# Down projection of the first three row tiles in three accumulation steps each, placed between the products of the inverse transform

## Chip, cores, metric

The kernel runs on one core of one Trainium2 chip. The metric is the device time of one execution in microseconds (us). A profile of one execution per kernel is read beside it; its span is some 2 us shorter than the device time. Within a group of runs the kernels share one chip and the runs of the kernel before.

## The reference

```
xn  = layernorm(x)                            # x: 2048 rows x 640, bf16
A   = irfft2(rfft2(xn) * (w_r + i w_i))       # over rows and columns
B   = ((xn @ w_gate) * (xn @ w_up)) @ w_down  # 640 -> 1536 -> 640
out = x + A + B
```

## The kernel before

The program is a list of tasks with priorities and dependences. A planner in the kernel's own code orders them on each engine at build time and hands out the eight PSUM banks (the buffers into which TensorE writes its sums; a bank is held until ScalarE or VectorE has read it, which is called an eviction where it is a copy); the chip then runs a fixed instruction stream per engine with semaphore waits. A lower priority number goes first; a task of lower priority may go ahead where the other can't start yet. Caps limit how many tasks of a class hold a bank at once.

The stages: layernorm and transposes (to some 20 us); the gate and up products, interleaved with the forward transform and then with the inverse transform along the rows (to some 140 us); the down projection, interleaved with the inverse transform along the columns (to the end). The tasks that the argument touches, cut:

```python
sch.caps = {"glu": 3, "acc": 3, ...}        # gate/up, down projection sums
...
ia = T("IA_%d" % q, "pe", ...)              # L1129, L1130: inverse row transform, 10 matmuls
ti = T("I_%d" % a, "pe", ...)               # L1158: inverse column transform, 5 matmuls, needs all of IA
# L1182 ... L1215: thirteen VectorE instructions per pair of row tiles (tasks V1 to V5)
...
def em_ag2(c, ...):                         # L1241: one sum of the down projection
    for ft in _FT_ORDER:                    # (7, 8, 9, 10, 11, 0, 1, 2, 3, 4, 5, 6)
        ins = c.e.matmul(ps[:, bk, ...], v_ht[:, ft, ...], v_wd[:, ft, sl3], start=(ft == 7 ...), stop=False)
ag2 = T("ACC_%d_%d" % (a, hf), "pe", 12 * ..., em_ag2,
        reads=[(b_ht, ...), (b_wd, None)],  # None: all of w_down
        prio=41 + ..., bank="single", cls="acc")
iv = T("IV_%d_%d", "pe", ..., after=[ag2])  # L1251: last product of a sum, needs V5
f1 = T("FIN_%d_%d", "dve", ..., frees=own, after=[iv])   # L1261: adds x, frees the bank
```

There are 16 row tiles of two halves (the last tile has three pieces), so 33 sums. w_down shares its memory with the table of the inverse row transform, apart from slices 7 to 11.

## Time and profile before

| | before |
|---|---|
| device time, median of the first runs | 207.04 us (206.98 to 207.76) |
| span of the profiled run | 205.3 us (this execution took 207.48) |
| TensorE, share busy | 97% |
| VectorE, share busy | 88% |
| TensorE time with nothing streaming, after the first transpose | 5.5 us: 4.9 in the pieces that the prediction lists, 0.6 in crumbs |

The distance between the starts of two matmuls, less what a fed stream takes (136 ns after one of 320 columns, 216 after 512): such gaps are called holes below. The wait that a profile line shows in brackets is smaller, since a matmul's record includes its pipeline.

### The profile page before, as it was taken

To read this page: it belongs to the slowest core of one execution; us is meant where nothing else is said; L and a number is where in the kernel's file an instruction comes from. 1 tells how busy PE (TensorE), PEld (TensorE's weight loads), DVE (VectorE), ACT (ScalarE), POOL (GpSimd) and SP (SyncE) were. 2 spreads that over 40 slices of the span, in tenths; PEclk is the share of its full clock that TensorE was granted. 3 is DMA by queue.
4 is the path that set the end of the run, shared out by engine and by line. 5 is a ranking of instruction groups with operands and counts; after the bars stand their busy time and mean duration, and the time that the engine had idled before them with its cause. 6 is when DMAs were issued, how large, how long until landed. Compare 5 with 4: busy or idle time off the path is not lost.

```text
span 205.3 us, 5062 instructions
## 1 busy us (share of the span) xinstructions
PE 198.4 (97%) x1925; PEld 134.9 (66%) x1925; DVE 179.7 (88%) x513; ACT 129.5 (63%) x287; POOL 32.2 (16%) x108
## 2 busy tenths in 40 slices
PE   7997999999999999899999999997999999999995
PEld 7897899545454555456666666656777777777774
DVE  3598999999999997697988889865999999999972
ACT  3687999999977676869999999987411220200000
POOL 0000000000000000075754575452000000000000
PEclk9999999999999999999999999999999999999999
DMA  6999963030351897405354534015122422243212
GB/s 182 299 337 382 361 80 64 3 64 0 64 69 36 247 201 203 128 0 133 74 149 104 130 81 118 0 16 159 55 60 84 117 80 67 80 112 111 82 50 64
DMA packets 31543, 23.83 MB, mean 116 GB/s; under 512 B 10528, under 2 KB 29472, under 8 KB 31392
## 3 DMA queue, kind: packets, MB, share of 16 engines
q1 hardware_dynamic: 30720, 23.16, 42.5%
q10 hardware_dynamic: 800, 0.36, 0.6%
q8 instruction: 15, 0.25, 0.5%
q14 instruction: 8, 0.07, 0.1%
HBM read 18.92 MB, written 2.62 MB: 105 GB/s over the span
## 4 chain that ended last, share of the span: by engine, by line
PE 89%; DVE 6%; DMA 1%; issue 1%; POOL 1%; ACT 0%; POOLq 0%
PE ps L977 37%; PE ps L1241 23%; PE ps L997 13%; PE ps L1129 3%; PE ps L1130 2%; PE ps L938 2%; PE ps L1251 2%; PE ps L1078 2%; PE ps L1055 2%; DVE arena L719 2%; PE ps L1158 2%; DMA arena<-in_A_x_dram 1%; PE ps L849 1%; PE ps L738 1%; DVE arena L785 0%
## 5 line engine op out<-in xcount | busy, mean ns | idle before, releaser
L718 ACT ACTIVATE arena<-ps 128x512 bf16<-128x512 f32 (+6 forms) x214 | 105.9, 534 | 40.5 <-PE ps L1158 25.3
L977 PE MATMUL ps<-arena 128*128 128x512 bf16 x360 | 84.1, 379 | 0.1
L977 PEld LDWEIGHTS ps<-arena 128*128 128x128 bf16 x360 | 33.2, 98 | 35.6 <-ACT arena L718 2.1
L1241 PE MATMUL ps<-arena 128*128 128x320 bf16 (+2 forms) x396 | 55.8, 295 | 0.0
L1241 PEld LDWEIGHTS ps<-arena 128*128 128x128 bf16 x396 | 37.9, 98 | 13.8
L997 PE MATMUL ps<-arena 128*128 128x128 bf16 (+1 forms) x360 | 28.0, 237 | 1.2 <-issue 1.1
L997 PEld LDWEIGHTS ps<-arena 128*128 128x128 bf16 x360 | 25.1, 98 | 3.2 <-issue 1.5
L1093 DVE TENSOR_TENSOR arena<-ps,arena 128x256 bf16<-128x256 f32 x64 | 24.0, 416 | 0.1
L1106 POOL TENSOR_SCALAR arena<-arena 128x256 bf16<-128x256 bf16 x8 | 6.8, 856 | 90.4 <-DVE arena L1096 90.4
L1013 DVE TENSOR_TENSOR arena<-arena 128x512 bf16<-128x512 bf16 x36 | 15.2, 422 | 5.0 <-ACT arena L718 4.9
L1261 DVE TENSOR_TENSOR arena<-ps,arena 128x320 bf16<-128x320 f32 (+2 forms) x33 | 15.5, 472 | 3.2 <-PE ps L1251 3.2
L719 DVE CAST arena<-ps 64x321 bf16<-64x321 f32 (+1 forms) x25 | 12.2, 490 | 6.3 <-PE ps L1130 5.9
L1129 PEld LDWEIGHTS ps<-arena 128*128 128x128 bf16 x160 | 12.4, 114 | 3.1 <-ACT arena L718 0.4
L1129 PE MATMUL ps<-arena 128*128 128x64 bf16 x160 | 13.3, 196 | 0.3 <-POOL arena L1115 0.3
L1130 PE MATMUL ps<-arena 128*128 128x64 bf16 x160 | 13.3, 197 | 0.0
L1130 PEld LDWEIGHTS ps<-arena 128*128 128x128 bf16 x160 | 11.2, 114 | 2.0
L1115 POOL TENSOR_SCALAR arena<-arena 128x65 bf16<-128x65 bf16 x32 | 12.0, 376 | 0.0
L1113 POOL COPY arena<-arena 128x63 bf16<-128x63 bf16 x32 | 8.7, 271 | 17.0 <-DVE arena L1096 16.8
L1096 DVE TENSOR_TENSOR arena<-ps,arena 128x130 bf16<-128x130 f32 x32 | 9.3, 291 | 0.0
L776 ACT ACTIVATE arena<-arena 128x640 bf16<-128x640 bf16 x11 | 9.1, 826 | 0.0
L1114 POOL COPY arena<-arena 128x63 bf16<-128x63 bf16 x32 | 8.9, 279 | 0.0
L891 DVE TENSOR_TENSOR arena<-arena 128x384 f32<-128x384 bf16 x16 | 8.8, 552 | 0.0
(63 smaller groups left out, 222.3 us busy)
## 6 DMA issues: line engine op xcount, KB each, us to landing
arena<-in_A_x_dram SPq DMA_DIRECT2D x20, 160.0 KB, 2.5
out_dram<-arena SPq DMA_DIRECT2D x31, 80.0 KB, 1.6
arena<-in_A_w_r_dram SPq DMA_DIRECT2D x8, 160.5 KB, 3.0
arena<-in_A_w_i_dram SPq DMA_DIRECT2D x8, 160.5 KB, 3.1
arena<-in_B_w_gate_dram SPq DMA_DIRECT2D x4, 320.0 KB, 5.6
arena<-in_A_x_dram SPq DMA_DIRECT2D x1, 1280.0 KB, 11.1
arena<-in_A_w_r_dram SPq DMA_DIRECT2D x14, 80.2 KB, 2.8
arena<-in_A_w_i_dram SPq DMA_DIRECT2D x14, 80.2 KB, 2.9
```

Source lines behind the costliest of these rows:

```text
L718: return c.e.activation(dst, src, _ACTF.Copy)
L719: return c.e.tensor_copy(dst, src)
L977: ins = c.e.matmul(ps[:, bk, :], v_gw[:, w, j, ft, :], v_xt[:, j, rows], start=(j == 0), stop=(j == 4))
L997: ins = c.e.matmul(ps[:, bk, w * n:(w + 1) * n], v_gw[:, w, j, ft, :], v_xt[:, j, rows], start=(j == 0), stop=(j == 4))
L1013: return c.e.tensor_tensor(v_ht[:, ft0, rows], v_gbf[:, rr, 0, :], v_gbf[:, rr, 1, :], _OP.mult)
L1093: c.e.tensor_tensor(dst, xh.unsqueeze(1).to_broadcast([128, 2, 32, 4]), wv, _OP.mult)
L1096: return c.e.tensor_tensor(d5, x5, wg[:, :, 0:321:5], _OP.mult)
L1115: return c.e.tensor_scalar(yg[:, 128:193], yg[:, 256:321], -1.0, None, _OP.mult)
L1129: c.e.matmul(dst, l1, v_ti[:, q, 0, :], start=True, stop=False)
L1130: ins = c.e.matmul(dst, l2, v_ti[:, q, 1, :], start=False, stop=True)
L1241: ins = c.e.matmul(ps[:, bk, 0:sl3.stop - sl3.start], v_ht[:, ft, a * 128:(a + 1) * 128], v_wd[:, ft, sl3], start=(ft == 7 and px is None) ...
L1261: return c.e.tensor_tensor(v_out[:, a % 2, sl3], ps[:, bk, 0:sl3.stop - sl3.start], v_xr[:, xs, sl3], _OP.add)
```

## The change

The intent: let the down projection of rows 0 to 2 fill TensorE's holes where the gate and up products have run out and the inverse transform waits for evictions. The diff, cut, without the removed branch for a preloaded x, which was never taken, and without the list of weight steps, which gives the same numbers as the old formula:

```diff
-        sch.caps = {"glu": opts.get("cap_glu", 3), "acc": opts.get("cap_acc", 3), "fill": 1}
+        sch.caps = {"glu": opts.get("cap_glu", 4), "acc": opts.get("cap_acc", 5), "fill": 1}
-            pf = opts.get("f_prio", 6.05) + 0.05 * g
+            pf = opts.get("f_prio", 5.8) + 0.05 * g
 ...
-                ag2 = T("ACC_%d_%d" % (a, hf), "pe", 12 * _d_mm(c1 - c0), em_ag2,
-                        reads=[(b_ht, ("col", a, a + 1)), (b_wd, None)], ...
+                cuts = (0, 5, 9, 12) if a < opts.get("acc_split", 3) else (0, 12)
+                own = ag2 = None
+                for k0, k1 in zip(cuts[:-1], cuts[1:]):
+                    def em_ag2(c, a=a, sl3=sl3, k0=k0, k1=k1, own=own):
+                        bk = bank_of(c.t) if own is None else bank_of(own)
+                        for ft in _FT_ORDER[k0:k1]:
+                            ins = c.e.matmul(..., start=(ft == _FT_ORDER[0]), stop=False)
+                    rd = [(b_wd, ("e", 640 * min(fts), 640 * (max(fts) + 1)))] if k1 - k0 < 12 else [(b_wd, None)]
+                    ag2 = T("ACC_%d_%d_%d" % (a, hf, k0), "pe", (k1 - k0) * _d_mm(c1 - c0), em_ag2, reads=[...] + rd, ...)
 ...
-                       prio=opts.get("iv_prio", 19.0) + ...
+                       prio=opts.get("iv_prio", 5.0) + ...
-        sch.urgent = ('T0_0', 'T0_1', 'T0_2', 'T0_3')
+        sch.urgent = ('T0_0', 'T0_1', 'T0_2', 'T0_3', 'sd_1', 'sd_2', 'sd_3')
```

More of the change, by code (lines that the diff above doesn't have):

```diff
@@ L958, in _build @@
                     q="act" if w_ and i < 1 else "sp")
-        w_at = [6.0 + opts.get("w_rate", 2.2) * min(ft // 2, 4) for ft in range(12)]
+        w_at = [6.0 + opts.get("w_rate", 2.2) * opts.get("w_step", (0, 1, 2, 3, 4, 4))[ft // 2] for ft in range(12)]
         c_at = [6.3 + opts.get("c_rate", 2.6) * (b0 + nb - 1) for b0, nb in _CHUNKS]
@@ L1228, in _build @@
                 sl3 = slice(c0, c1)
-                pre = a >= opts.get("x_pre", 16)
-                px = None
-                if pre:
-                    def em_px(c, xs=xs, sl3=sl3):
-                        return c.e.activation(ps[:, bank_of(c.t), 0:sl3.stop - sl3.start], v_xr[:, xs, sl3], _ACTF.Copy)
-                    px = T("PX_%d_%d" % (a, hf), "act", _d_act(c1 - c0), em_px, reads=[(b_xr, ("r", xs, xs + 1))],
-                           prio=pc + 0.001 * hf, bank="single", cls="acc")
@@ L1237, in em_ag2 @@
-                def em_ag2(c, a=a, sl3=sl3, px=px):
-                    bk = bank_of(c.t) if px is None else bank_of(px)
-                    ins = None
-                    for ft in _FT_ORDER:
-                        ins = c.e.matmul(ps[:, bk, 0:sl3.stop - sl3.start], v_ht[:, ft, a * 128:(a + 1) * 128],
-                                         v_wd[:, ft, sl3], start=(ft == 7 and px is None), stop=False)
-                    return ins
-                kw = dict(bank="single", cls="acc") if px is None else dict(after=[px])
@@ L1245, in _build @@
-                ag2 = T("ACC_%d_%d" % (a, hf), "pe", 12 * _d_mm(c1 - c0), em_ag2,
-                        reads=[(b_ht, ("col", a, a + 1)), (b_wd, None)],
-                        prio=pc + 0.01 + 0.001 * hf, **kw)
-                own = ag2 if px is None else px
+                cuts = (0, 5, 9, 12) if a < opts.get("acc_split", 3) else (0, 12)
[3 more added lines that the diff above has]
+                        bk = bank_of(c.t) if own is None else bank_of(own)
+                        ins = None
+                        for ft in _FT_ORDER[k0:k1]:
+                            ins = c.e.matmul(ps[:, bk, 0:sl3.stop - sl3.start], v_ht[:, ft, a * 128:(a + 1) * 128],
+                                             v_wd[:, ft, sl3], start=(ft == _FT_ORDER[0]), stop=False)
+                        return ins
+                    kw = dict(bank="single", cls="acc") if own is None else dict(after=[ag2])
+                    fts = _FT_ORDER[k0:k1]
+                    rd = [(b_wd, ("e", 640 * min(fts), 640 * (max(fts) + 1)))] if k1 - k0 < 12 else [(b_wd, None)]
+                    ag2 = T("ACC_%d_%d_%d" % (a, hf, k0), "pe", (k1 - k0) * _d_mm(c1 - c0), em_ag2,
+                            reads=[(b_ht, ("col", a, a + 1))] + rd,
+                            prio=pc + 0.01 + 0.001 * hf + opts.get("acc0_prio", 0.0) * (a < opts.get("acc_split", 3)), **kw)
+                    own = own or ag2
@@ L1254, in _build, with em_f1 @@
                        reads=[(b_v, ("a", a, a + 1)), (b_sm, ("t", 1, 3))],
-                       prio=opts.get("iv_prio", 19.0) + 0.05 * a + 0.01 + 0.001 * hf, after=[ag2])
-                def em_f1(c, own=own, a=a, xs=xs, sl3=sl3, pre=pre):
+                       prio=opts.get("iv_prio", 5.0) + 0.05 * a + 0.01 + 0.001 * hf, after=[ag2])
+                def em_f1(c, own=own, a=a, xs=xs, sl3=sl3):
                     bk = bank_of(own)
-                    if pre:
-                        return copy_on(c, v_out[:, a % 2, sl3], ps[:, bk, 0:sl3.stop - sl3.start])
                     return c.e.tensor_tensor(v_out[:, a % 2, sl3], ps[:, bk, 0:sl3.stop - sl3.start], v_xr[:, xs, sl3],
                                              _OP.add)
-                f1 = T("FIN_%d_%d" % (a, hf), ("act", "dve") if pre else "dve",
-                       {"dve": _d_dve_psum(c1 - c0), "act": _d_act(c1 - c0)}, em_f1,
-                       reads=[] if pre else [(b_xr, ("r", xs, xs + 1))], writes=[(b_out, rb[0])],
+                f1 = T("FIN_%d_%d" % (a, hf), "dve", _d_dve_psum(c1 - c0), em_f1,
+                       reads=[(b_xr, ("r", xs, xs + 1))], writes=[(b_out, rb[0])],
                        prio=opts.get("fin_prio", 41.0) + 0.05 * a - 0.001, frees=own, after=[iv])
@@ L1270, in _build @@
         sch.window = 100.0
-        sch.urgent = opts.get("urgent", ('T0_0', 'T0_1', 'T0_2', 'T0_3'))
+        sch.urgent = opts.get("urgent", ('T0_0', 'T0_1', 'T0_2', 'T0_3', 'sd_1', 'sd_2', 'sd_3'))
         sch.slack["act"] = opts.get("slack_act", 700.0)
```

## The prediction

> **What bounds the kernel now.** I read the busy shares of the page first, then the chain that ended last, then the table by stretches of 10 us, then the order of time around each hole in TensorE's row, and last VectorE's row from 140 us to the end. By source line: L997 and L977 are the gate and up products, L1129 and L1130 the inverse row transform, L1158 the inverse column transform, L1182 to L1215 its VectorE part, L1241 the down projection, L1251 the last product added to it, L1261 the addition of x.
>
> Page, parts 1 and 4:
>
> ```profile
> PE 198.4 (97%) x1925; PEld 134.9 (66%) x1925; DVE 179.7 (88%) x513; ACT 129.5 (63%) x287; POOL 32.2 (16%) x108
> ...
> PE 89%; DVE 6%; DMA 1%; issue 1%; POOL 1%; ACT 0%; POOLq 0%
> ```
>
> TensorE is 97% busy and is 89% of the chain. But a matmul's record here includes its pipeline: a 320-column one is recorded as 299 ns while the next starts 136 ns after it. So I took the distances between starts, and subtracted the record less 163 ns, which is what a fed stream shows (216 ns for 512 columns, 136 for 320, 56 for 128, about 30 for 64). What remains is TensorE time with no work streaming. After the first transpose at 5.55 us it is 4.9 us in all: 0.7 in pieces of 0.08 to 0.23 before 15 us; 1.29 at 16.43; 0.71 at 86.32; 0.31 at 94.74; 0.43, 0.78, 0.12 and 0.30 between 139.9 and 142.9; 0.27 at 148.94; the rest in crumbs. From 149 us to 203.0 there is none. Everything else is products that the change keeps.
>
> TensorE in order of time:
>
> ```profile
> 139.96 0.19 PE L1129 MATMUL ps<-arena 128*128 128x64 bf16 x1 [0.27 <-POOL arena L1115]
> ...
> 141.06 2.28 PE L1158 MATMUL ps<-arena 128*128 128x128 bf16 x30 [0.62 <-ACT arena L718]
> 143.22 3.42 PE L1241 MATMUL ps<-arena 128*128 128x320 bf16 x24
> ```
>
> This is the seam between two stages. The gate and up products, which filled the holes of the inverse transform, run out at 139.2 us (the group of ten at 137.04). What is left waits for GpSimd, then for ScalarE's eviction, then for two evictions more inside the 30. The down projection could fill it, but its first matmul stands at 143.22, because each of its tasks asks for all of w_down. That weight shares its memory with the inverse transform's table, so its last slice (160 KB) is issued at 140.48, after the last L1130, and lands at 142.69. The first 800 KB (slices 7 to 11, which share nothing) landed at 82.01; slices 0 to 3 by 127.43; 4 and 5 at 139.96.
>
> The stretches, and VectorE in order of time; columns of the first are busy us of PE, PEld, DVE, ACT, POOL, then clock and DMA:
>
> ```profile
> 130.00:140.00 10.00, 9.73 (x113) 5.91 (x110) 7.39 (x24) 8.87 (x22) 5.57 (x19) 1.00 0.13 34
> 140.00:150.00 10.00, 9.13 (x94) 6.82 (x95) 8.19 (x19) 5.15 (x9) 0.00 (x0) 1.00 0.29 84
> 150.00:160.00 10.00, 10.00 (x88) 7.50 (x87) 10.00 (x26) 2.07 (x4) 0.00 (x0) 1.00 0.30 83
> 160.00:170.00 10.00, 10.00 (x82) 7.38 (x80) 9.97 (x24) 1.83 (x3) 0.00 (x0) 1.00 0.32 91
> ```
>
> ```profile
> 142.10 0.82 DVE L719 COPY arena<-ps 128x640 f32<-128x640 f32 x1 [1.65 <-PE ps L1158]
> ...
> 199.43 0.89 DVE L1261 TENSOR_TENSOR arena<-ps,arena 128x320 bf16<-128x320 f32 x2 [1.29 <-PE ps L1251]
> 201.34 0.49 DVE L1261 TENSOR_TENSOR arena<-ps,arena 128x320 bf16<-128x320 f32 x1 [1.01 <-PE ps L1251]
> 202.38 0.36 DVE L1261 TENSOR_TENSOR arena<-ps,arena 128x192 bf16<-128x192 f32 x1 [0.55 <-PE ps L1251]
> 203.03 0.29 DVE L1261 TENSOR_TENSOR arena<-ps,arena 128x128 bf16<-128x128 f32 x1 [0.30 <-PE ps L1251]
> ```
>
> From 142.10 to 198.14 VectorE has no hole over 0.06 us; only the last four waits, 1.29 + 1.01 + 0.55 + 0.30 = 3.15 us, are slack. So the last stage is nearly two-bound. VectorE finishes a pair of rows every 7.0 us (its last step, L1215, starts at 148.47, 155.49, 162.51, ...), and TensorE's work for a pair is 4 x 13 x 0.136 = 7.07 us.
>
> **What the Trainium skill says.** "Perfetto Trace Analysis", Identifying the Most-Contended Engine: matmul busy share is no good measure of headroom on the tensor engine. The trace agrees (299 ns recorded against 136 ns of spacing), hence the count by starts. The same page, Optimization Strategy: where the most-contended engine changes over time, interleaving the stages may help, and the gaps on that engine are the place to look. That is what this change tries. "TensorE: Matmul & The Clock Gate", Step-by-step: a warm stream spaces matmuls by N/2.4 + 2.5 ns, 135.8 for 320 columns; the trace has 136. "PSUM — Partial Sum Buffer", The four PSUM rules: a sum may be continued later, since only a first matmul clears marks in its own bank. So cutting a group of twelve in three, with each sum in a bank of its own, adds no matmul; the bank is only held longer. No run has shown that yet.
>
> **The change part by part.**
> - *Down projection of rows 0, 1, 2 (six sums) in steps of 5, 4 and 3 matmuls, each asking only for its own slices.* Work added: none; 6 x 12 = 72 matmuls x 0.136 = 9.8 us stay. A step of 5 (0.68 us) can run any time after 82 us, one of 4 (0.54 us) after 127.4, one of 3 (0.41 us) only after 142.7.
> - *Sums in flight 3 to 5.* Before 142.7 us up to 5 x 9 x 0.136 = 6.1 us of filler is thus allowed, against holes of 0.43 + 0.78 + 0.12 + 0.30 = 1.63 us. The fillers come last in priority, so they go where nothing else can start. The later hole of 0.27 is a wait for the first VectorE pair (148.9) with all three banks filled: two more banks close it too. Sum: 1.63 + 0.27 = 1.9 us off TensorE's path.
> - *Gate/up cap 3 to 4.* One more bank for the filler of the middle stage. At most the holes at 86.32 and 94.74, 1.0 us; these follow waits for VectorE's evictions and are where the planner may not have foreseen them. ScalarE is 9.6 of 10 us busy there, so more gate/up products in flight mostly queue for it. I count 0.2.
> - *Priority of the forward transform 6.05 to 5.8.* In the old numbering it already stands just ahead of the layernorm group that it doesn't depend on, and VectorE is 9.7 to 10.0 of 10 us busy from 20 to 80 us either way. I count 0.
> - *Three square roots made urgent.* ScalarE starts them 0.02 to 0.2 us after their input already (7.14, 10.89, 13.36). I count 0. The hole of 1.29 us at 16.43 has no releaser in the profile and the change does not aim at it.
> - *Last product's priority 19 to 5.* It runs as soon as its data are there; this frees a bank sooner. 0 by itself.
> - *The list of weight steps* gives the same numbers as the old formula, and the removed branch for a preloaded x was never taken (its threshold is 16, rows go to 15). 0.
>
> Subtract: up to 0.5 us because an inverse transform's product that becomes ready while a step of 0.41 to 0.68 us runs must wait for it, half of one on average, and because five held banks of eight leave fewer pairs of banks for L1158. That delays VectorE's start at 142.9, not TensorE. VectorE's own floor is 203.0 - 3.15 = 199.9 us for the start of the last addition, plus 0.5 for this delay = 200.4; TensorE's is 203.0 - 1.9 - 0.2 = 200.9. TensorE still decides, narrowly; I take 0.2 off for the friction. Net gain 1.9 + 0.2 - 0.2 = 1.9 us: 207.04 - 1.9 = 205.1.
>
> **Rivals.**
> 1. VectorE becomes the bound. For it: rates of 7.0 and 7.07 us per pair, 10.00 busy. If the new order starts the first pair a microsecond later, the end is 199.9 + 1.0 + friction and the gain shrinks to about 1: 206.0. Against: 3.15 us of slack.
> 2. Five held sums starve the middle stage. If fillers slip in from 86 us on, each keeps its bank until 149 us; 5 of 8 gone leaves 3 for gate/up and transform, and TensorE waits for evictions. That could cost 1 to 3 us: 206 to 208. Against: fillers stand behind the gate/up products, and TensorE is full in 97 to 137 us, so few holes call them.
> 3. The middle stage gains as well. All of the 1.0 us at 86 and 95, and an inverse chain that ends earlier since fillers need no eviction: gain about 3 us, 204.0. Beyond that VectorE's 3.15 us stop it.
> 4. The order of the first 17 us changes by luck of the re-planning: plus or minus 1 us.
>
> **Range and chances.** Best guess 205.1. Rivals 1 and 2 make the upper side, 206.5; rival 3 with luck at the start the lower, 203.8. Faster by over 2% needs under 202.9, 4.1 us, which is nearly all idle time that I can find and more than VectorE's slack, so it takes an earlier VectorE start as well: 4%. Slower by over 2% needs over 211.2: 2%.
>
> **What would show it.** Right: down-projection steps of 5 and 4 between the transform products before 142 us, no hole over 0.2 us in TensorE's starts from 137 to 150 us, the same 1925 matmuls, the last additions waiting for TensorE by under 3.15 us in all. Wrong: the first L1182 of the new kernel over a microsecond later with VectorE full to the end (rival 1); new waits of L977 for evictions between 90 and 137 us (rival 2); or a changed start of the forward transform, which I count as nothing.

## The result, and the profile after

The changed kernel took 205.01 us in the median (204.64 to 205.58, four runs) against 207.09. The ratio was 0.9895, with a 95% interval of 0.9864 to 0.9927. A ratio is the mean time of one kernel's runs over that of the other's of the same rounds, so it is not quite the ratio of the medians quoted. In a later group of five rounds the same two kernels stood at 205.05 and 206.41 us, ratio 0.993 (0.9913 to 0.9946). By the medians the gain is 2.1 us in the first group and 1.4 us in the second; the intervals of both allow 1.5 to 1.8 us. The forecast was 1.9 us and 205.1.

The line numbers of the changed kernel differ from the kernel before past L1226: L1236 is the down projection (was L1241), L1248 the last product (was L1251), L1256 the addition of x (was L1261).

Page, parts 1 and 4, after:

```profile
PE 197.5 (97%) x1908; PEld 134.8 (66%) x1925; DVE 179.5 (88%) x513; ACT 129.5 (64%) x287; POOL 31.9 (16%) x108
...
PE 67%; DVE 20%; DMA 4%; SPq 4%; issue 2%; ACT 2%
```

The shares don't tell the two kernels apart. The number of weight loads is the same, 1925; that only 1908 matmuls are shown is 17 records of L977 missing from this trace, each of which looks like a false gap of 0.215 us and is left out of all sums. The chain now runs through VectorE for 20% instead of 6%. That does not make VectorE the bound: the run with less VectorE work, below, is not faster beyond the noise. The shares also vary for one stream (TensorE 89% in the profile of the kernel before, 82% in the control's).

TensorE in order of time after the change, at the seam between the stages (the start of a piece, its length, engine, line, what it does, how many):

```profile
138.48 0.84 PE L1236 MATMUL ps<-arena 128*128 128x320 bf16 x5
...
139.49 0.71 PE L1236 MATMUL ps<-arena 128*128 128x320 bf16 x4
140.27 1.00 PE L1158 MATMUL ps<-arena 128*128 128x128 bf16 x15
141.10 0.84 PE L1236 MATMUL ps<-arena 128*128 128x320 bf16 x5
141.78 0.44 PE L1158 MATMUL ps<-arena 128*128 128x128 bf16 x5
142.06 0.71 PE L1236 MATMUL ps<-arena 128*128 128x320 bf16 x4
```

The three lines of before have become six. The steps of 5 and 4 of the two halves of row 0 stand in front of and between the products, and no wait is bracketed any more. Of the four holes, 1.63 us in all, 0.24 us is left, before the 15 at 140.27: the filler was finished and the last eviction was not. The hole of 0.27 us before the first last product is gone too. Before, and after:

```profile
148.94 0.58 PE L1251 MATMUL ps<-arena 128*128 128x320 bf16 x3
```

```profile
148.47 0.71 PE L1248 MATMUL ps<-arena 128*128 128x320 bf16 x4
```

But 20 us later there is a new one. ScalarE, TensorE and VectorE, after:

```profile
159.70 1.30 ACT L718 ACTIVATE arena<-ps 128x640 f32<-128x640 f32 x2 [6.73 <-PE ps L1158]
...
163.04 0.71 PE L1248 MATMUL ps<-arena 128*128 128x320 bf16 x4
...
163.47 0.49 DVE L1256 TENSOR_TENSOR arena<-ps,arena 128x320 bf16<-128x320 f32 x1
...
164.03 1.80 PE L1236 MATMUL ps<-arena 128*128 128x320 bf16 x12 [0.28 <-DVE arena L1256]
```

Four last products run at 163.04, VectorE's first addition ends and frees a bank at 163.96, and only then does the next sum start: a hole of 0.44 us. The cap of five is not what stops it. By then 12 sums are complete and eight additions are done, so four sums hold banks; the other four banks were emptied by ScalarE's evictions of L1158, which ended at 161.0. The planner did not use them. For a single bank its code prefers one whose neighbour is held (`pen = 0.0 if partner[0] is None else 1.0`) over one that comes free earlier. Its plan, rebuilt from the kernel's code and not visible in a trace, puts the next sum in the bank that this addition frees.

So the seam and what follows it gained 1.63 - 0.24 + 0.27 - 0.44 = 1.22 us. The two profiles differ by 205.3 - 203.1 = 2.2 us. The remaining 1.0 us lies before 24 us, where the two streams are nearly the same: the first group of ten L938 starts at 23.36 us before and at 22.33 after. Before:

```profile
14.80 0.50 PE L997 MATMUL ps<-arena 128*128 128x128 bf16 x6
16.43 2.74 PE L997 MATMUL ps<-arena 128*128 128x128 bf16 x45 [1.13 <-issue]
```

In the changed kernel's profile this hole isn't there. Comparing the two built programs shows what can differ at all. On every engine the streams are the same up to the last ten L1130, but for one place: near 13 us the urgent square root sd_3 stands before one eviction on ScalarE, and two VectorE instructions change places. Raising the gate/up cap, the forward transform's priority and the last product's priority changed no instruction: with any one of them set back, the changed kernel's program is the same.

The VectorE end of the last stage, after:

```profile
198.73 1.67 DVE L1256 TENSOR_TENSOR arena<-ps,arena 128x320 bf16<-128x320 f32 x4 [1.30 <-PE ps L1248]
200.70 0.29 DVE L1256 TENSOR_TENSOR arena<-ps,arena 128x128 bf16<-128x128 f32 x1 [0.30 <-PE ps L1248]
```

Its slack at the end shrank from 3.15 to 1.60 us.

### The profile page after: what moved, and what is told of

It is laid out like the page before. It is cut to its first block, busy times and chain, and to the rows that moved or that the text cites. A ratio compares the mean times of both kernels' runs of the same rounds, so it can differ in the third digit from the quotient of the medians.

```text
span 203.1 us, 5045 instructions
## 1 busy us (share of the span) xinstructions
PE 197.5 (97%) x1908; PEld 134.8 (66%) x1925; DVE 179.5 (88%) x513; ACT 129.5 (64%) x287; POOL 31.9 (16%) x108
## 4 chain that ended last, share of the span: by engine, by line
PE 67%; DVE 20%; DMA 4%; SPq 4%; issue 2%; ACT 2%
PE ps L1236 26%; PE ps L977 24%; DMA arena<-in_A_x_dram 4%; SPq L712 4%; PE ps L997 3%; PE ps L1130 2%; PE ps L1078 2%; PE ps L1129 2%; PE ps L1158 2%; PE ps L1248 2%; DVE arena L1013 2%; PE ps L1055 2%; DVE arena L902 2%; DVE arena L891 2%; DVE arena L892 1%
## 5 line engine op out<-in xcount | busy, mean ns | idle before, releaser
L977 PE MATMUL ps<-arena 128*128 128x512 bf16 x343 | 81.0, 379 | 1.0
L977 PEld LDWEIGHTS ps<-arena 128*128 128x128 bf16 x360 | 33.1, 98 | 35.6 <-ACT arena L718 2.1
L1236 PE MATMUL ps<-arena 128*128 128x320 bf16 (+2 forms) x396 | 55.8, 295 | 0.3 <-DVE arena L1256 0.3
L1236 PEld LDWEIGHTS ps<-arena 128*128 128x128 bf16 x396 | 37.6, 98 | 14.0 <-DVE arena L1256 0.6
L997 PE MATMUL ps<-arena 128*128 128x128 bf16 (+1 forms) x360 | 28.1, 237 | 0.0
L997 PEld LDWEIGHTS ps<-arena 128*128 128x128 bf16 x360 | 24.9, 98 | 2.2 <-ACT arena L718 0.5
L1256 DVE TENSOR_TENSOR arena<-ps,arena 128x320 bf16<-128x320 f32 (+2 forms) x33 | 15.4, 472 | 1.6 <-PE ps L1248 1.6
L1130 PE MATMUL ps<-arena 128*128 128x64 bf16 x160 | 13.3, 197 | 0.0
L1130 PEld LDWEIGHTS ps<-arena 128*128 128x128 bf16 x160 | 11.2, 113 | 2.1
```

What stands on the lines that cost most here:

```text
L977: ins = c.e.matmul(ps[:, bk, :], v_gw[:, w, j, ft, :], v_xt[:, j, rows], start=(j == 0), stop=(j == 4))
L997: ins = c.e.matmul(ps[:, bk, w * n:(w + 1) * n], v_gw[:, w, j, ft, :], v_xt[:, j, rows], start=(j == 0), stop=(j == 4))
L1130: ins = c.e.matmul(dst, l2, v_ti[:, q, 1, :], start=False, stop=True)
L1236: ins = c.e.matmul(ps[:, bk, 0:sl3.stop - sl3.start], v_ht[:, ft, a * 128:(a + 1) * 128], v_wd[:, ft, sl3], start=(ft == _FT_ORDER[0]), st ...
L1256: return c.e.tensor_tensor(v_out[:, a % 2, sl3], ps[:, bk, 0:sl3.stop - sl3.start], v_xr[:, xs, sl3], _OP.add)
```

## The experiments

Two theories for the 2.2 us between the profiles. Theory A: the seam gives about 1.2 us, and the altered start removes a hole that belongs to the old order. Theory B: the hole at 16.43 us is chance, and the rest of the change must account for everything. Twelve kernels ran, in three groups of four, five rounds each.

### The control: two parts that change no instruction

```diff
 kernel before
-"cap_glu", 3   "f_prio", 6.05
+"cap_glu", 4   "f_prio", 5.8
```

> The kernel before with two parts of the change put in, the gate/up cap at 4 and the forward transform's priority at 5.8. The planner gives the same instruction stream on every engine, so all theories expect a ratio of 1.000 within 0.003. It is the control, and a second look at the hole of 1.29 us at 16.43 us: if the hole belongs to the stream (theory A) it is there again, at 1.1 to 1.4 us in TensorE's starts near 16.4 us; if it is chance of one execution (theory B) it is gone or lies elsewhere.

206.63 us against 206.52, ratio 1.0001 (0.9986 to 1.0016). TensorE in order of time in this run, where the kernel before had the hole:

```profile
14.83 3.39 PE L997 MATMUL ps<-arena 128*128 128x128 bf16 x54
```

The same stream ran on without the stop; its first L938 stands at 22.37 us, as in the changed kernel. So the hole of 1.29 us does not belong to the stream but to one execution (or to its chip, since the two profiles are of different groups), and the profile pair exaggerates the change by about 1 us. On one chip, too, the start varies: this run and the run without the new start, below, have the same stream up to 138 us, and their first L938 stands at 22.37 and 22.92 us. Theory A falls in that point.

The DMA records of the traces hold a candidate that the waits don't show. The first packet of the kind "instruction" on queue 8 (16 KB) after the start stands at 14.07 us in the profile of the kernel before and at 11.34 us in this one. Of the other twelve profiles, five have it at 12.8 to 13.1 us, and four of these have a hole of 0.35 to 0.62 us between two L997 from 15.3 to 15.7 us; seven have it before 12 us, and none of these has such a hole over 0.10 us from 15 to 17 us. No run tests it, so it is not shown as the cause.

### The start alone

```diff
 kernel before
-sch.urgent = (..., 'T0_3')
+sch.urgent = (..., 'T0_3', 'sd_1', 'sd_2', 'sd_3')
```

> The kernel before with only the three urgent square roots. The streams differ in one place: sd_3 on ScalarE comes before one gate/up eviction, and VectorE's two products of that time come after the scaling. Theory A (the old order is what makes the hole at 16.43 us): no hole there, 1.0 us faster, ratio 0.995. Theory B (chance): the same as the control, ratio 1.000. My prediction counted this part as 0, as theory B does.

206.31 us, ratio 0.9986 (0.997 to 1.0002). Its profile had two large holes near the start, 0.41 at 14.22 and 0.79 us at 15.58. The measured effect is 0.3 us; the interval reaches from none to 0.6 us, so it is not separated from zero.

### Everything but the start

```diff
 changed kernel
-sch.urgent = (..., 'T0_3', 'sd_1', 'sd_2', 'sd_3')
+sch.urgent = (..., 'T0_3')      # and cap_glu 3, f_prio 6.05
```

> The changed kernel with the old start (and with the old gate/up cap and forward priority, which change no instruction). What stays is the cut sums, their own slices, and five sums in flight. Theory A: 1.1 to 1.2 us faster than the kernel before, ratio 0.9943, and 1.0 us slower than the changed kernel. Theory B: all of the change's 2.1 us, ratio 0.990. The seam from 137 to 143 us reads as in the changed kernel, with TensorE holes of about 0.25 us instead of 1.63.

205.26 us, ratio 0.9938 (0.9922 to 0.9955): 1.3 us. The holes are 0.24 at 140.85 and 0.44 us at 164.6. The seam's account of 1.22 us from the profile and the measured 1.3 us agree. Theory B's ratio of 0.990 lies outside the interval, so B falls in its second half.

### Cut, but three sums in flight

```diff
 changed kernel
-"cap_acc", 5
+"cap_acc", 3
```

> The changed kernel with at most three sums in flight. The stream to the seam and through it is the same as the changed kernel's, since only the two sums of row 0 are used as filler there; after it the order differs. If the larger cap is worth what my prediction gave it, a hole of about 0.3 us comes back before the first last product near 148 us, and the kernel is 0.3 us slower than the changed one (ratio to before 0.991). If three sums leave TensorE without work until the first VectorE pair is done, the hole is 1 to 1.5 us and the ratio 0.995 to 0.997. If the hole of 0.44 us at 164 us in the changed kernel comes of having five sums open, it is gone here.

206.39 us, ratio 0.9998 (0.9979 to 1.0017). The seam was filled exactly as in the changed kernel, with one hole of 0.24 us. Yet nothing was gained. TensorE:

```profile
145.36 1.11 PE L1236 MATMUL ps<-arena 128*128 128x320 bf16 x7
148.29 0.58 PE L1248 MATMUL ps<-arena 128*128 128x320 bf16 x3 [1.82 <-DVE arena L1215]
```

A hole of 1.98 us stands before 148.29. The first VectorE pair is ready then, not sooner, and until it is no sum can be completed and no bank freed. Three sums are 36 matmuls; those that ran in the seam are missing here. The filler did not shorten the path, it moved the idle time from the seam to this wait. It takes the two more sums of the larger cap, 24 matmuls of 0.136 us or 3.3 us of work, to fill it. The hole at 164 us is gone here, as expected.

### Unaltered, for comparison within a group

> The changed kernel unaltered, for comparison within this group and as a second look. If the parts add, the ratio to before is 0.9938 x 0.9986 = 0.9924 (1.6 us); if the first measurement of 0.9895 (2.2 us) is right to the last tenth, about 0.9895. The holes at the seam and at 164 us belong to the stream and must come again: 0.24 near 140 and 0.44 near 164 us. The holes before 24 us should differ from the first look, since they differed between executions of one stream already.

205.05 us against 206.41, ratio 0.993 (0.9913 to 0.9946). The two holes came back: 0.24 at 140.27, 0.44 us at 164.03. The product of the parts, 0.9938 x 0.9986 = 0.9924, lies inside this interval and inside the first one.

### Uncut, five sums in flight

```diff
 changed kernel
-cuts = (0, 5, 9, 12) if a < 3 else (0, 12)
+cuts = (0, 12)
```

> The changed kernel with its sums uncut (one step of twelve that asks for all of w_down), five sums in flight, urgent square roots kept. If the cutting is what fills the seam, TensorE has the four holes of 1.63 us in all between 138 and 143 us again, only the hole of 0.27 us near 148 us is gone, and the kernel gains 0.2 to 0.3 us from that and about 0.3 from the start: ratio 0.997. If five sums in flight alone carry the gain (rival, suggested by the run with three, where the cut gained nothing), the ratio is 0.993.

206.05 us, ratio 0.9985 (0.9963 to 1.0008). The four holes are back (0.43, 0.78, 0.12 and 0.31 us from 139 to 142 us), that of 0.27 at 148 is gone, a small one of 0.12 us at 163.5 is new. So the larger cap alone is worth next to nothing, and so is the cut alone (the run with three sums): only both together gain.

### Cut, but each step asks for all of w_down

```diff
 changed kernel
-rd = [(b_wd, ("e", 640 * min(fts), 640 * (max(fts) + 1)))] if k1 - k0 < 12 else [(b_wd, None)]
+rd = [(b_wd, None)]
```

> The changed kernel with its steps of 5, 4 and 3, but each step asking for all of w_down again. If it is the slices that let the filler in, the seam has its 1.63 us of holes again and the ratio is 0.998 as with uncut sums. If smaller steps alone help, holes of under 1 us and a ratio of 0.995.

206.09 us, ratio 0.9977 (0.9955 to 0.9999). The seam:

```profile
139.98 2.28 PE L1158 MATMUL ps<-arena 128*128 128x128 bf16 x30 [0.62 <-ACT arena L718]
142.14 2.47 PE L1236 MATMUL ps<-arena 128*128 128x320 bf16 x17
```

This is the picture of before: the 30 together, with their wait. The steps alone do not fill the seam; that each asks for its own slices lets them in.

### Steps of 5, 6 and 1

```diff
 changed kernel
-cuts = (0, 5, 9, 12) if a < 3 else (0, 12)
+cuts = (0, 5, 11, 12) if a < 3 else (0, 12)
```

> The changed kernel with steps of 5, 6 and 1 instead of 5, 4 and 3, so that the filler before the first L1158 is 0.27 us longer, against a hole of 0.24 there. If that hole waits only for the eviction, it shrinks to under 0.1 and the kernel gains 0.1 to 0.2 us over the changed one, provided VectorE's slack at the end (1.6 us) holds. If VectorE decides the end by now, nothing is gained.

205.20 us, ratio 0.9937 (0.9921 to 0.9952), so no better than the changed kernel of the same group. The hole at 140 us was filled, as hoped. In its place a hole of 0.22 us appeared at 152.19, where a sum waits for a bank, and that of 164 stayed at 0.46. Again idle time moved to the next wait for a bank.

### The same with less VectorE work (wrong on purpose)

The moved holes suggested that VectorE sets the pace of the last stage: it has no hole there, and frees the banks.

```diff
 steps of 5, 6 and 1
-                c.e.tensor_tensor(v_vb[:, b_:b_ + 2, 5:10:2, :], ..., _OP.subtract)
-                return c.e.tensor_tensor(v_vb[:, b_:b_ + 2, 1:5:2, :], ..., _OP.subtract)
+                return c.e.tensor_tensor(v_vb[:, b_:b_ + 2, 5:10:2, :], ..., _OP.subtract)
```

> Wrong on purpose: the run with steps of 5, 6 and 1, less one VectorE addition of 0.34 us in each of the eight pairs (L1215 of the changed kernel, 2.7 us in all), the order of everything else kept. It asks whether VectorE decides the last stage as well. If TensorE's holes of 0.22 at 152 and 0.46 at 164 us are waits for banks that a late VectorE frees, both vanish and the kernel is 0.5 to 0.7 us faster than that run, though no TensorE work was removed: ratio to before 0.990 to 0.991. If they come of something else, they stay and the ratio stays at 0.9935.

205.02 us against 206.71, ratio 0.992 (0.9903 to 0.9936; the interval overlaps that of the run before, in another group), and a wrong result as intended. TensorE and VectorE:

```profile
162.95 0.71 PE L1247 MATMUL ps<-arena 128*128 128x320 bf16 x4
163.39 0.49 DVE L1255 TENSOR_TENSOR arena<-ps,arena 128x320 bf16<-128x320 f32 x1 [0.56 <-PE ps L1247]
...
163.93 1.80 PE L1235 MATMUL ps<-arena 128*128 128x320 bf16 x12 [0.28 <-DVE arena L1255]
```

(Lines are one lower in this kernel.) VectorE now idles 0.56 us, waiting for TensorE's last products, and TensorE still waits for VectorE's addition: the hole is 0.44 us as before, and that at 152 is 0.22. The expectation failed in its first half. The hole isn't VectorE's load, it is a round trip. In TensorE's fixed order the four last products stand behind 24 matmuls of two other sums, and the next sum was planned into the bank that the first of those four frees, as above: 163.93 - 162.95 = 0.98 us from the first last product to the next sum, of which four products cover 0.54. Four other banks are free at that time, so another choice of bank could avoid the wait. In the planner with the preference for held neighbours taken out, the plan has no wait at this sum; no such kernel was run.

### A better version, first attempt: more cuts, and the addition earlier

```diff
 changed kernel
-"acc_split", 3
+"acc_split", 16
 # V1, four VectorE instructions, cut into two tasks of two, the first after V5 of the pair before
```

> An attempt at a better kernel: the changed one with all sums cut in 5, 4 and 3, and with VectorE's first task of a pair cut in two, so that the addition of x (which frees a bank) can stand two instructions earlier. If the hole of 0.44 us at 164 us comes of TensorE waiting for a bank while VectorE does four instructions of the next pair, it falls under 0.1 us and the kernel gains 0.3 to 0.4 us over the changed one. If additions placed earlier push VectorE's pairs back and the last pair decides the end, the gain is 0 or less.

207.24 us, ratio 1.0026 (1.0009 to 1.0044). The two parts were not tried one by one. The hole at 164 us is gone, but there are three others of the same kind (L1244 is the down projection here, L1264 the addition):

```profile
171.95 2.48 PE L1244 MATMUL ps<-arena 128*128 128x320 bf16 x17 [0.28 <-DVE arena L1264]
180.01 5.74 PE L1244 MATMUL ps<-arena 128*128 128x320 bf16 x41 [0.26 <-DVE arena L1264]
194.69 5.81 PE L1244 MATMUL ps<-arena 128*128 128x320 bf16 x45 [0.39 <-DVE arena L1264]
```

They are 0.44, 0.42 and 0.55 us: the plan waits for a bank that an addition frees more often. At each of the three only four sums hold banks in the rebuilt plan, and two pairs of banks are free.

### Held banks on purpose

```diff
 changed kernel
-opts.get("acc0_prio", 0.0)
+opts.get("acc0_prio", -1.5)     # cut sums ahead of the gate and up products
```

> Rival 2 of my prediction on purpose: the cut sums of rows 0 to 2 get priority over the gate and up products, so five of them start near 77 us and keep their banks to the end of the transform. If held banks starve the middle stage, TensorE shows many new waits for evictions between 85 and 137 us and the kernel is 2 to 6 us slower than the changed one (ratio to before 1.002 to 1.02). If three banks suffice, it is within 0.5 us of the changed one.

252.95 us, ratio 1.2244, far outside what I expected. TensorE, and the stretch from 100 to 120 us (columns as in the prediction):

```profile
80.81 3.72 PE L1236 MATMUL ps<-arena 128*128 128x320 bf16 x15 [2.91 <-DMA arena<-in_B_w_down_dram]
```

```profile
100.00:120.00 20.00, 12.89 (x155) 8.98 (x156) 12.20 (x41) 12.46 (x29) 8.84 (x33) 0.50 0.37 93
```

The first sums even waited for their weights. The first steps of five sums, 25 matmuls, ran from 80.81 to 86.4 us, and no last product ran before 166.9, so five of eight banks were held in between. From 100 to 120 us TensorE was busy 12.9 of 20 us, and the clock granted to it fell to 0.50: matmuls of 64 columns (L1055) stood 53 ns apart there, 29 in the kernel before. The last term I had not reckoned with at all. How much of the loss is held banks, weights, order or clock is not separated.

### A better version, second attempt: one step ahead, one bank held

```diff
 changed kernel
 # first step of the first sum: priority 9.0 instead of 41, after the fourth group of L1055
```

> A second attempt at a better kernel: only the first step of the first sum is put ahead, right after the fourth group of L1055 near 83.5 us, against the hole of 0.70 us before L1078 at 85.3 us; one bank is then held from there. If the middle stage can spare one bank and its pace is TensorE's, the hole is gone and VectorE's last stage starts 0.3 to 0.7 us earlier: 0.3 to 0.7 us faster than the changed kernel, ratio to before 0.990. If ScalarE and the chain set the pace of the middle stage, VectorE's last stage starts when it did and nothing is gained.

217.65 us with one slow execution, 217.4 without, ratio 1.0516. (Lines are one higher in this kernel: L1079 is L1078 of the others.) The step ran at 83.20 us, too early for the hole at 85.3 us, which wasn't filled (0.95 us shown before L1079 now), and new waits followed. TensorE, then two stretches:

```profile
91.23 0.19 PE L1130 MATMUL ps<-arena 128*128 128x64 bf16 x1 [1.13 <-POOL arena L1116]
...
97.53 0.69 PE L1079 MATMUL ps<-arena 128*128 128x321 bf16 x2 [1.01 <-ACT arena L718]
```

```profile
90.00:95.00 5.00, 3.38 (x83) 2.99 (x82) 3.49 (x12) 4.50 (x12) 3.50 (x13) 1.00 0.50 122
95.00:100.00 5.00, 3.00 (x31) 1.67 (x29) 4.88 (x16) 4.46 (x11) 3.09 (x11) 0.74 0.31 79
```

The clock fell to 0.74 between 95 and 100 us. The planner made another order of the whole middle stage out of this one step, so whether the held bank or the order costs the 10.7 us over the kernel before is not separated. No version tried beats the changed kernel.

## Why the prediction was right

The time was right: 205.1 forecast, 205.01 and 205.05 measured, the whole range of the runs inside 203.8 to 206.5. The mechanism was right too: partial sums fill the seam. That the time agrees to a tenth is partly luck. The forecast gain of 1.9 us stands on terms of which the runs confirm 1.2 to 1.3 us; the start adds 0.3 us that is not separated from zero; and the kernel before, from which the 1.9 were subtracted, was 0.3 to 0.6 us faster in the later groups than in the first. Step by step:

- **The seam's holes and why the filler could not get in.** Right, and shown: with slices the filler enters; asked for all of w_down, it doesn't, and the 1.63 us return. The cut sums come out correct.
- **"1.63 + 0.27 = 1.9 us off TensorE's path."** Over-sized. 1.66 us were taken off (0.24 stayed, over the 0.2 that the prediction named as its sign), and 0.44 came back at 164 us as a wait for a bank: 1.22 us by the profile, 1.3 by the run without the start.
- **"Two more banks close it too", 0.27 us.** Right for the hole before the first last product, but the term was mis-sized in its role. With three banks the whole gain is lost (1.98 us of hole, ratio 0.9998). I counted filled holes as time off the path; the filler is work taken from the stretch up to 148 us, where the sums can't be completed before VectorE's first pair. The larger cap is the condition of the gain, not an extra.
- **0.2 us in the middle stage from the gate/up cap.** Wrong: it changed no instruction, and the holes before L1078 (0.71 us) and near 94 us (0.31) are as before; rival 3's gain in the middle stage did not come either. The working also misread a line: ScalarE's 9.6 of 10 us is the stretch from 100 us on; around the two holes it is 7.84 (80 to 90 us) and 8.99 (90 to 100).
- **0 for the forward priority, the last product's priority and the step list.** Right, by identical programs. **0 for the square roots.** Not refuted; 0.3 us is measured, with an interval that includes 0.
- **0.2 us of friction, and TensorE deciding narrowly before VectorE.** The delay of VectorE's start, for which up to 0.5 us was allowed, was 0.2: the first L1182 stands 119.75 us after the first L938, 119.51 before. The friction on TensorE was another thing, the hole at 164 us, 0.44, which comes of the planner's choice of bank and which the prediction did not foresee. That VectorE isn't the bound is shown by its idling once an instruction is taken from each pair while TensorE's holes stay. Rival 1 falls in that form.
- **Rival 2, starving the middle stage, at 1 to 3 us.** It did not happen: with fillers last in priority, the streams are the same up to the last ten L1130. Forced, with the sums put first, it cost 46 us over the kernel before instead of 1 to 3; the share of the held banks in that is not separated.
- **Rival 4, luck of the re-planning at the start, plus or minus 1 us.** The size came, the mechanism didn't: the planned order hardly changed, and it is executions of one stream that differ, by 1 us between two profiles.
- **A sum.** The pieces listed under "4.9 us in all" make 4.91 without the crumbs; with them it is 5.5. Nothing rests on it.

What stays open: why the first group gave 0.9895 and the second 0.993. The intervals overlap, and the kernel before took 207.09 us in the first and 206.4 to 206.7 in the others. The varying start and the chip are candidates, not shown for those runs.

## What to carry to other kernels

Filler in a hole gains only if the stage that it was taken from has other work for that time: count how far the next wait is, and how many open sums reach it, before counting the hole as gain. Let each partial step wait for its own slice of a shared buffer, and give fillers the lowest priority, since every started sum holds its bank until its last input exists. When an engine waits for a buffer, count how many are free at that moment before blaming the cap or the engine that frees it. Before explaining a difference between two profiles, profile the same instruction stream twice and compare the built streams.

## What the Trainium skill lacked or had wrong

- "TensorE: Matmul & The Clock Gate", Back-to-back issue gap, gives as sustained roofline of weight load and matmul pairs about 81 ns at 128 columns and 131 ns at 512, and calls N/2.4 + 2.5 ns the isolated gap. Here, with as many weight loads as matmuls (360 and 360 for L977), the sustained spacing is 216 ns at 512 columns, 136 at 320 and 56 at 128: the formula holds, the roofline figures don't.
- "TensorE: Matmul & The Clock Gate", HAM oscillation, puts the abstract rule at idle gaps over about 3.4 us. The part after it, A second HAM failure mode: psum-queue depth-cycling, adds that frequent short ones can do it as well, without a number. Here the mean granted clock fell to 0.74 from 95 to 100 us in the last run, whose longest TensorE hole up to then was 1.3 us and whose TensorE was busy 3.4 of 5 us just before, and to 0.50 from 100 to 120 us in the run with five held banks, whose longest hole there was 1.7 us.
- No page found gives the round trip of a PSUM bank from a last product on TensorE over VectorE's addition to the next sum: 0.98 us here, 0.44 of it not covered by other products.
- No page found says that an identical stream may stop for 1.29 us near its start in one execution and not in another, with no releaser in the profile's waits.
